# Zero rows for the last token block of attention, and a new order of work, in an attention and two-MLP kernel

## The chip, the cores and the metric

The kernel runs on one core of a Trainium2 chip. The metric is the time of one execution on the device, in microseconds (us), the median of several runs.

## What is computed

Forgetting attention on 4 batches, 8 heads, 576 tokens and 64 dimensions a head, then two MLPs on the 2304 tokens:

```python
scores = scale * np.matmul(q, k.transpose(0, 1, 3, 2))
cum = np.cumsum(np.log(np.clip(f, 0.0001, 1.0)), axis=-1)
scores = np.where(causal, -1000000000.0, scores + cum[:, :, :, None] - cum[:, :, None, :])
attn = np.exp(scores - np.max(scores, axis=-1, keepdims=True))
attn = attn / (np.sum(attn, axis=-1, keepdims=True) + 1e-09)
x = np.matmul(attn, v)                                    # to 2304 tokens x 512
h = x @ w_in;   x = (np.maximum(h, 0) + alpha * np.minimum(h, 0)) @ w_out
h = x @ w_in2;  x = (np.maximum(h, 0) + np.log1p(np.exp(-np.abs(h)))) @ w_out2
```

The MLPs are 512 to 2048 to 512. All is float32; the kernel splits operands into a high and a low float32r part and adds three products.

## The kernel before

576 tokens are four blocks of 128 and one of 64. Heads are taken two at a time, so a pair (`pairs`, 16 of them) fills 128 partitions. For each pair SP loads q, k and v by token blocks (`load_tok`, L468 and L472, where L472 brings the last block, into rows 0 to 63). `transposed` (L497) turns q and k, in two halves (`prep_q`, `prep_k`): blocks 0 and 1, then blocks 2, 3 and the short one, whose transpose reads 64 rows. GpSimd makes the high and low parts of v (`prep_v`, L558 and L562). `query_tile` takes 64 queries of both heads: the decay on GpSimd (L578), scores on TensorE (L592; for the first eight pairs in float32, with a mask product L595), row maximum on VectorE (L601), exponential on ScalarE (L614), the transposes of the probabilities (L625) and their high (ScalarE, L641) and low parts (VectorE, L645), which lie in blocks of the tiles `PT` (p00, p01, p10, p11, with h or l). `values` multiplies them by v (L680), for queries 0 to 255 and 256 to 575 and for each head: token block by token block, the high part and then the low one. In the second of these the last two of ten products read the short block, again 64 rows. `finish` divides by the sums and hands the result on, through DRAM for batches 2 and 3 (L744).

The MLPs work on six chunks of 384 tokens. `hidden` (L816) makes 128 rows of h with 12 products, `product` (L873) multiplies by w_out, `weights` loads (L382, L387, or a saved copy, L368) and splits the weights on ScalarE and VectorE (L390 to L416). Chunks 0 to 2 (batches 0 and 1) are worked on with the first MLP beside the last eight pairs; at the end of attention (`switch2`) its memory becomes that of chunks 3 to 5, which `fetch` brings from DRAM (L776: x3h, x4h, x5h and x3l, x4l, x5l).

The order of all work comes from a planner, `Plan`: each step is added with its engine, an assumed length, what it reads and writes, and a rank; `emit` plays the steps through and gives each engine, of those that are ready, the one of least rank. The ranks come from the numbers in `TUNE`: a unit per query tile (`TILE1`, `TILE2`), per MLP slot (`SLOT2`, `SLOT3`), and offsets for each kind of step, one for the first eight pairs and one for the last eight. The program then holds a fixed order on each engine; waits between engines are by semaphores.

## Time and profile before

| | us |
|---|---|
| median of 3 runs (lowest, highest) | 1051.91 (1050.93, 1052.27) |
| the profiled execution | 1050.04 |
| its span in the profile | 1048.1 |
| TensorE (PE) busy | 1036.1 (99%) |
| VectorE (DVE) busy | 731.8 (70%) |
| ScalarE (ACT) busy | 539.0 (51%) |
| GpSimd (POOL) busy | 220.8 (21%) |

Busy times are unions over the whole span; what they mean is seen only by stages, as the shares differ between attention alone, attention beside the first MLP, and the MLPs alone. In a timeline the start of a TensorE instruction is recorded, its end is modelled, and neighbours overlap: what an instruction costs is read from the distance between its start and the next one.

### The profile page before, as it was taken

How to read it: one execution, taken by the hardware profiler on the slowest of the kernel's cores; microseconds unless marked ns; L12 is line 12 of the kernel's file. 1: busy time of each engine (PE TensorE's matmuls, PEld its weight loads, DVE VectorE, ACT ScalarE, POOL GpSimd, SP SyncE). 2: the span in 40 equal slices, each digit the busy share in tenths (PEclk: the TensorE clock that was granted, in tenths of full speed). 3: DMA queues.
4: the chain of work that ended last, by engine and by line, in shares of the span. 5: the costliest groups of instructions: out<-in, count | busy, mean ns of one | idle time of the engine just before them, and what ended most of it. 6: DMA issues, size and time to landing. Idle time of an engine off the chain costs nothing.

```text
span 1048.1 us, 16749 instructions
## 1 busy us (share of the span) xinstructions
PE 1036.1 (99%) x5852; PEld 955.9 (91%) x5852; DVE 731.8 (70%) x1664; ACT 539.0 (51%) x1312; POOL 220.8 (21%) x399
## 2 busy tenths in 40 slices
PE   8999999999999999999999999999999999999998
PEld 6777779999999999999999999999999999999997
DVE  6899888897999887532334669736954895495453
ACT  6899887777777654443333356334522442242221
POOL 6787755564345410000000000000000000000000
PEclk8999999999999999999999999999999999999999
DMA  6656345554564359003131203101300130010111
GB/s 147 145 143 182 92 138 161 173 171 139 171 194 144 103 155 300 2 11 111 61 121 61 81 1 101 61 1 33 114 16 1 42 105 15 1 41 3 58 52 69
DMA packets 125923, 97.49 MB, mean 93 GB/s; under 512 B 82496, under 2 KB 103120, under 8 KB 125840
## 3 DMA queue, kind: packets, MB, share of 16 engines
q1 hardware_dynamic: 125840, 96.43, 31.2%
q8 instruction: 46, 0.75, 0.3%
q14 instruction: 37, 0.30, 0.1%
HBM read 74.24 MB, written 22.17 MB: 92 GB/s over the span
## 4 chain that ended last, share of the span: by engine, by line
PE 92%; DVE 4%; ACT 2%; issue 1%; DMA 1%; POOL 0%; SPq 0%; DVEq 0%; ACTq 0%
PE h L816 37%; PE o L873 37%; PE pt L592 6%; PE pt L680 5%; PE pt L625 4%; PE pt L497 1%; DVE d L601 0%; DMA raw<-in_moe_w_in_dram 0%; ACT p L614 0%; DVE p01l L645 0%; DVE ca L405 0%; ACT qw L538 0%; DVE ca L401 0%; DMA kr<-in_k_dram 0%; DVE acc L894 0%
## 5 line engine op out<-in xcount | busy, mean ns | idle before, releaser
L873 PE MATMUL o<-g,wout 128*128 128x384 f32 x1152 | 214.9, 336 | 0.2 <-DVE x4l L905 0.2
L873 PE MATMUL o<-wout,g 128*128 128x512 f32 x864 | 214.5, 393 | 0.0
L873 PEld LDWEIGHTS o<-g,wout 128*128 128x128 f32 x1152 | 199.9, 188 | 1.0 <-DVE x4l L905 0.5
L873 PEld LDWEIGHTS o<-wout,g 128*128 128x128 f32 x864 | 160.8, 188 | 29.4
L855 DVE TENSOR_TENSOR g<-h,g 128x384 fp32r<-128x384 f32 x192 | 106.5, 555 | 56.0 <-ACT g L852 55.5
L842 ACT ACTIVATE ta<-ta 128x384 f32<-128x384 f32 x96 | 50.4, 525 | 175.2 <-DVE ta L838 175.1
L852 ACT CAST g<-h 128x384 fp32r<-128x384 f32 x192 | 92.0, 480 | 91.0 <-DVE h L845 52.4
L829 DVE SCALAR_TENSOR_TENSOR h<-ta,slope,h 128x384 f32<-128x384 f32 x96 | 59.4, 618 | 77.2 <-ACT h L826 77.0
L578 POOL TENSOR_SCALAR d<-cumb,cumc 128x64 f32<-128x64 f32 (+2 forms) x144 | 91.5, 640 | 101.6 <-ACT p L614 88.2
L838 DVE TENSOR_SCALAR ta<-h 128x384 uint32<-128x384 uint32 x96 | 53.3, 555 | 69.7 <-PE h L816 69.6
L823 ACT ACTIVATE ta<-h 128x384 f32<-128x384 f32 x96 | 47.1, 491 | 105.0 <-PE h L816 104.2
L614 ACT ACTIVATE p<-d,mx 128x64 f32<-128x64 f32 (+2 forms) x144 | 80.9, 562 | 13.2 <-DVE mx L601 12.2
L894 DVE TENSOR_TENSOR acc<-o,acc 128x512 f32<-128x512 f32 (+1 forms) x102 | 62.7, 622 | 20.3 <-PE o L873 18.3
L845 DVE SCALAR_TENSOR_TENSOR h<-h,ta 128x384 f32<-128x384 f32 x96 | 54.0, 563 | 31.6 <-ACT ta L842 31.6
L601 DVE CUSTOM_DVE_ANT_0 d<-pt,d 128x64 f32<-128x64 f32 (+2 forms) x144 | 63.3, 450 | 7.9 <-PE pt L592 2.2
L625 PE MATMUL pt<-ident,p 128*128 128x128 f32 (+1 forms) x400 | 64.3, 281 | 2.3 <-DVE p01l L645 0.8
L625 PEld LDWEIGHTS pt<-ident,p 128*128 128x128 f32 (+1 forms) x400 | 45.1, 140 | 12.7 <-ACT p L614 4.1
L816 PE MATMUL h<-x0h,win 128*128 128x384 f32 x256 | 55.5, 339 | 0.0
L816 PE MATMUL h<-x1h,win 128*128 128x384 f32 x256 | 55.4, 339 | 0.0
L816 PE MATMUL h<-x2h,win 128*128 128x384 f32 x256 | 55.2, 338 | 0.0
L816 PE MATMUL h<-x5h,win 128*128 128x384 f32 x256 | 54.9, 335 | 0.0
L816 PE MATMUL h<-x4h,win 128*128 128x384 f32 x256 | 54.9, 335 | 0.0
(138 smaller groups left out, 1966.8 us busy)
## 6 DMA issues: line engine op xcount, KB each, us to landing
raw<-in_moe_w_in_dram SPq DMA_DIRECT2D x32, 512.0 KB, 4.6
raw<-in_moe_w_out_dram SPq DMA_DIRECT2D x32, 512.0 KB, 3.5
rb<-rd SPq DMA_DIRECT2D x32, 144.0 KB, 3.7
out_dram<-acc SPq DMA_DIRECT2D x18, 256.0 KB, 2.0
cumb<-cum_d SPq DMA_DIRECT2D x30, 144.0 KB, 3.3
qr<-in_q_dram SPq DMA_DIRECT2D x32, 128.0 KB, 2.5
kr<-in_k_dram SPq DMA_DIRECT2D x32, 128.0 KB, 2.5
vr<-in_v_dram SPq DMA_DIRECT2D x32, 128.0 KB, 3.6
```

What stands on the lines that cost most here:

```text
L578: nc.gpsimd.tensor_scalar(out=buf(dk)[:, 0:w], in0=buf(cb)[:, 0:w], scalar1=-1.0, scalar2=cumc[:, t, i:i + 1], op0=ALU.mult, op1=ALU.add,)
L592: nc.tensor.matmul(out=buf(key)[:, 0:c1 - c0], lhsT=a[:, t, :], rhs=b_[:, c0:c1], start=(s == 0), stop=(s == len(products) - 1 and not mas ...
L601: nc.vector.tensor_tensor_reduce(out=d[:, c0:c1], in0=buf(key)[:, 0:c1 - c0], in1=d[:, c0:c1], scale=-1.0, scalar=least, op0=ALU.add, op1= ...
L614: nc.scalar.activation(out=buf(pk)[:, 0:w], in_=buf(dk)[:, 0:w], func=AF.Exp, bias=buf(mk)[:, x:x + 1], scale=-1.0, accum_out=buf(sm)[:, t ...
L625: nc.tensor.transpose(out=buf(tk[x])[0:rows, (j - j0) * 128:(j - j0) * 128 + 128], in_=buf(pk)[:, j * 128:j * 128 + rows], identity=ident,)
L816: nc.tensor.matmul(out=hb(), lhsT=w_[:, kk * 128:kk * 128 + 128], rhs=x_[:, kk, :], start=(s == 0), stop=(s == len(ops) - 1))
L829: nc.vector.scalar_tensor_tensor(out=hb(), in0=buf(ka), scalar=slope[:, ff:ff + 1], in1=hb(), op0=ALU.mult, op1=ALU.add)
L845: nc.vector.scalar_tensor_tensor(out=hb(), in0=hb(), scalar=0.0, in1=buf(ka), op0=ALU.max, op1=ALU.add)
L852: nc.scalar.copy(out=buf(kg)[0], in_=hb())
L855: nc.vector.tensor_sub(buf(kg)[1], hb(), buf(kg)[0].bitcast(F32))
L873: nc.tensor.matmul(out=buf(ok)[:, 0:width], lhsT=a, rhs=b_, start=(j == 0 and s == 0), stop=(j == G - 1 and s == 2))
L894: nc.vector.tensor_add(buf(ok)[:, 0:width] if inner else ac(), buf(ok)[:, 0:width], ac())
```

## The change

The short block is filled up: rows 64 to 127 of the last block of the loaded q and k, as before of v, and of the block of `PT` that holds the short block's probabilities are set to zero once, at the start; loads and evictions only ever write rows 0 to 63 there. The transposes of q and k and the value products then read 128 rows for every block. The transpose of the short block writes 128 columns, of which 64 are read on. The planner's assumed lengths of transposes, scores and value products are altered, and all numbers of `TUNE` are new, so most steps stand elsewhere in each engine's order.

```diff
-    "TILE1": 0.34, "TILE2": 2.84, "SLOT2": 14.32, "SLOT3": 1.72, "qr": (-39.24, -10.94), "kr": (-19.35, 4.31),
...
+    "TILE1": 2.64, "TILE2": 2.56, "SLOT2": 25.17, "SLOT3": 1.95, "qr": (-2.51, -15.17), "kr": (3.69, -1.2),
...
@@ transposed
         for c in range(c0, c1):
-            n = min(128, S - c * 128)
             nc.tensor.transpose(
-                out=p[:, c * 128 - t0:c * 128 - t0 + n],
-                in_=src[0:n, c].rearrange("p h d -> p (h d)"),
-                identity=ident[0:n, 0:n],
+                out=p[:, c * 128 - t0:c * 128 - t0 + 128],
+                in_=src[:, c].rearrange("p h d -> p (h d)"),
+                identity=ident,
             )
@@ prep_k, and the same in prep_q
-        plan.add("pe", (c1 - c0) * 0.1075, lambda: transposed(pk, buf(rk), hf), writes=[pk] + ([key] if hf == 0 else []),
-                 reads=[rk, ("ident",)] + ([key] if hf else []), rank=rank)
+        plan.add("pe", (c1 - c0) * 0.109 + 0.04, lambda: transposed(pk, buf(rk), hf), writes=[pk] + ([key] if hf == 0 else []),
+                 reads=[rk, ("ident",), ("vz",)] + ([key] if hf else []), rank=rank)
@@ query_tile
-        plan.add("pe", sum(t_f32(c1 - c0) if whole(i) else 3 * t_mm(c1 - c0) for c0, c1 in cuts) + 0.06 * whole(i), scores,
+        plan.add("pe", sum(t_f32(c1 - c0) if whole(i) else 3 * t_mm(c1 - c0) for c0, c1 in cuts) + 0.06 * whole(i) + 0.04, scores,
...
-            plan.add("pe", (j1 - j0) * 0.1075, lambda x=x: turn(x), reads=[pk], writes=[tk[x], region], rank=R(n + due("turn", i)))
+            plan.add("pe", (j1 - j0) * 0.109 + 0.04, lambda x=x: turn(x), reads=[pk], writes=[tk[x], region], rank=R(n + due("turn", i)))
@@ values
                 for s, (j, x, c0) in enumerate(mm):
-                    rows = min(128, S - j * 128)
                     b0, nt = block((i0 + c0) // 64, j), (w - c0) // 64
                     nc.tensor.matmul(
                         out=buf(pk)[:, c0:w],
-                        lhsT=buf(vk)[0:rows, j, h].rearrange("p a d -> p (a d)"),
-                        rhs=PT[home(i)][g][x][0:rows, b0:b0 + nt, h, :],
+                        lhsT=buf(vk)[:, j, h].rearrange("p a d -> p (a d)"),
+                        rhs=PT[home(i)][g][x][:, b0:b0 + nt, h, :],
...
-            plan.add("pe", sum(t_mm(w - c0) for _, _, c0 in mm), pe, rank=R(n0 + h),
-                     reads=[vk] + regions + ([] if g == h == 0 else [yk]),
+            plan.add("pe", sum(t_mm(w - c0) for _, _, c0 in mm) + 0.04, pe, rank=R(n0 + h),
+                     reads=[vk, ("pz",)] + regions + ([] if g == h == 0 else [yk]),
@@ setup
-        plan.add("pool", 0.15, lambda: zero(tiles["vr", 0][64:128, NJ - 1]), writes=[("vz",)], rank=R(-8))
+        for x in ("qr", "kr", "vr"):
+            plan.add("pool", 0.15, lambda x=x: zero(tiles[x, 0][64:128, NJ - 1]), writes=[("vz",)], rank=R(-8))
+        for n in range(2):
+            for x in range(2):
+                plan.add("pool", 0.15, lambda n=n, x=x: zero(PT[n][1][x][64:128, 15].bitcast(F32)), writes=[("pz",)], rank=R(-6))
```

Three places show what moved.

TensorE, late in the first pair and early in the second (L497 becomes L496: transposes of q and k; L625 becomes L624: of probabilities; L592 becomes L591: scores). Before:

```order
L625 MATMUL pt5_0_156<-ident_60,p3_0_150 128x128 x4
L592 MATMUL pt7_0_158<-kw0_0_161,qw0_0_159 128x384
L595 LDWEIGHTS identb_61
L595 MATMUL pt7_0_158<-maskb_63,identb_61 128x64
L497 MATMUL pt0_0_116<-ident_60,qr0_0_124 128x128 x2
L625 MATMUL pt1_0_117<-ident_60,p0_0_110 128x128 x2
L497 MATMUL pt2_0_118<-ident_60,kr0_0_125 128x128 x2
L497 MATMUL pt4_0_155<-ident_60,qr0_0_124 128x128 x2
L497 MATMUL pt4_0_155<-ident_60,qr0_0_124 128x64
L497 MATMUL pt3_0_119<-ident_60,kr0_0_125 128x128 x2
L497 MATMUL pt3_0_119<-ident_60,kr0_0_125 128x64
```

and now, a little earlier in the first pair:

```order
L624 MATMUL pt5_0_156<-ident_60,p3_0_150 128x128
L591 MATMUL pt6_0_157<-kw0_0_161,qw0_0_159 128x512
L594 LDWEIGHTS identb_61
L594 MATMUL pt6_0_157<-maskb_63,identb_61 128x64
L496 MATMUL pt7_0_158<-ident_60,qr0_0_124 128x128 x2
L624 MATMUL pt0_0_116<-ident_60,p0_0_110 128x128
L591 MATMUL pt1_0_117<-kw0_0_161,qw0_0_159 128x256
L594 LDWEIGHTS identb_61
L594 MATMUL pt1_0_117<-maskb_63,identb_61 128x64
L496 MATMUL pt2_0_118<-ident_60,qr0_0_124 128x128 x3
L624 MATMUL pt4_0_155<-ident_60,p1_0_111 128x128 x4
```

The transposes of the second pair's q stand between the first pair's scores instead of behind them, and the second half is three full transposes instead of two and one of 64 columns.

SP, at the end of attention: the last two stores to DRAM (L744, now L742), the fetch of chunks 3 to 5 (L776, now L774) and weight loads. Before, and then now:

```order
L744 DMA xb_dh_67<-rb0_0_134 128x576
L744 DMA xb_dl_68<-x320_0_107 128x576
L368 DMA win5_0_4721<-w_dh_69 128x512
L368 DMA win5_1_4722<-w_dl_70 128x512
L776 DMA x3h_4711<-xb_dh_67 128x4x384
L776 DMA x4h_4713<-xb_dh_67 128x4x192 x2
L776 DMA x5h_4715<-xb_dh_67 128x4x384
L382 DMA raw1_0_84<-in_moe2_w_in_dram 128x4x128
L368 DMA wout0_0_1863<-w_dh_69 128x512
L368 DMA wout0_1_1864<-w_dl_70 128x512
L776 DMA x3l_4712<-xb_dl_68 128x4x384
L368 DMA wout1_0_1865<-w_dh_69 128x512
```

```order
L742 DMA xb_dh_67<-rb0_0_134 128x576
L742 DMA xb_dl_68<-x320_0_107 128x576
L382 DMA raw1_0_84<-in_moe2_w_in_dram 128x4x128
L368 DMA win5_0_4889<-w_dh_69 128x512
L368 DMA win5_1_4890<-w_dl_70 128x512
L774 DMA x3h_4879<-xb_dh_67 128x4x384
L774 DMA x4h_4881<-xb_dh_67 128x4x192 x2
L774 DMA x5h_4883<-xb_dh_67 128x4x384
L368 DMA wout5_0_4891<-w_dh_69 128x512
L368 DMA wout5_1_4892<-w_dl_70 128x512
L774 DMA x3l_4880<-xb_dl_68 128x4x384
L774 DMA x4l_4882<-xb_dl_68 128x4x192 x2
```

A load of w_in2 (L382) now stands between the stores and the first fetch, and one pair of w_out loads instead of a w_in2 load and a pair between x5h and x3l. That load needs its buffer raw1 free of an earlier read, which is the last of these rows of VectorE (the L689 are the sums of the last value products, L405 the read of raw1; the L892 add results of TensorE):

```order
L689 TENSOR_TENSOR x320_0_107<-pt2_0_118,xt_133 64x320
...
L689 TENSOR_TENSOR x320_0_107<-pt0_0_116,xt_133 64x320
L853 TENSOR_TENSOR g4_1_1893<-h0_0_1898,g4_0_1892 128x384
L827 SCALAR_TENSOR_TENSOR h1_0_1899<-ta1_0_1897,slope_64,h1_0_1899 128x384
L393 TENSOR_SCALAR cu0_0_87<-ca0_0_85 128x512
L892 TENSOR_TENSOR o0_0_1900<-o0_0_1900,acc0_1881 128x384
L397 SCALAR_TENSOR_TENSOR cu0_0_87<-raw1_0_84,cu0_0_87 128x512
L853 TENSOR_TENSOR g5_1_1895<-h1_0_1899,g5_0_1894 128x384
L892 TENSOR_TENSOR o1_0_1901<-o1_0_1901,acc0_1881 128x384
L401 TENSOR_SCALAR ca0_0_85<-raw1_0_84 128x512
L405 SCALAR_TENSOR_TENSOR ca0_0_85<-ca0_0_85,raw1_0_84 128x512
```

GpSimd, at the start, behind the mask (the first decays are L578, now L577; L558 and L562 become L557 and L561). Before, and then now, with some rows of the zeroing left out of the second:

```order
L976 MEMSET vr0_0_126 64x128
L976 MEMSET qw0_0_159 128x1152
L976 MEMSET qw1_0_160 128x1152
L976 MEMSET q0_0_120 128x1152
L976 MEMSET q0_1_121 128x1152
L610 MEMSET p3_0_150 128x64
L558 TENSOR_SCALAR v0_0_106<-vr0_0_126 128x5x64
L578 TENSOR_SCALAR d3_0_148<-cumb0_0_105,cumc_65 128x64
L578 TENSOR_SCALAR d0_0_108<-cumb0_0_105,cumc_65 128x128
L578 TENSOR_SCALAR d1_0_109<-cumb0_0_105,cumc_65 128x576
```

```order
L974 MEMSET qr0_0_124 64x128
L974 MEMSET qw0_0_159 128x1152
L974 MEMSET kr0_0_125 64x128
L974 MEMSET p01h_114 64x128
...
L974 MEMSET q0_1_121 128x1152
L557 TENSOR_SCALAR v0_0_106<-vr0_0_126 128x5x64
L609 MEMSET p3_0_150 128x64
L561 TENSOR_TENSOR v0_0_106<-vr0_0_126,v0_0_106 128x5x64
L557 TENSOR_SCALAR v0_0_106<-vr0_0_126 128x5x64
L561 TENSOR_TENSOR v0_0_106<-vr0_0_126,v0_0_106 128x5x64
L577 TENSOR_SCALAR d3_0_148<-cumb0_0_105,cumc_65 128x64
```

Six memsets are added, and all of the first pair's v work stands ahead of the first decays. In SP's queue the first pair's v is now loaded before its k.

## Rows read from the trace of the kernel before

**Rows 1.** The page, busy time of the engines and share of the span.

```profile
PE 1036.1 (99%) x5852; PEld 955.9 (91%) x5852; DVE 731.8 (70%) x1664; ACT 539.0 (51%) x1312; POOL 220.8 (21%) x399
```

**Rows 2.** Busy times by stretch; the second number of an engine counts its instructions.

```profile
core 0: us, PE busy (x) PEld busy (x) DVE busy (x) ACT busy (x) POOL busy (x), PEclk, DMA share, GB/s
0.00:26.00 26.00, 23.35 (x129) 17.62 (x130) 16.98 (x52) 16.20 (x45) 16.02 (x38) 0.87 0.63 147
26.00:131.00 105.00, 102.63 (x654) 79.39 (x652) 94.36 (x295) 93.88 (x284) 83.08 (x144) 1.00 0.56 141
76.80:92.40 15.60, 14.77 (x95) 11.33 (x96) 14.88 (x47) 14.59 (x44) 13.09 (x23) 1.00 0.67 182
131.00:145.00 14.00, 11.60 (x71) 9.02 (x69) 12.17 (x38) 10.80 (x33) 9.70 (x20) 1.00 0.51 141
145.00:384.00 239.00, 238.44 (x1500) 228.01 (x1499) 214.36 (x537) 176.01 (x457) 108.68 (x196) 1.00 0.53 155
```

**Rows 3.** Order of time on PE, end of a group of value products: start, length, instruction.

```profile
62.89 0.27 PE L680 MATMUL pt<-p01l,v 128*128 128x192 f32 x1
63.09 0.29 PE L680 MATMUL pt<-p01h,v 64*128 64x64 f32 x1
...
63.43 0.41 PE L680 MATMUL pt<-p01h,v 128*128 128x320 f32 x1
63.68 0.30 PE L680 MATMUL pt<-p01l,v 128*128 128x320 f32 x1
```

**Rows 4.** Order of time on PE, three 64-column products with 128 rows.

```profile
183.30 0.50 PE L592 MATMUL pt<-k,q 128*128 128x64 f32 x3
183.64 0.60 PE L816 MATMUL h<-x1h,win 128*128 128x384 f32 x2
```

**Rows 5.** Order of time on PE, transposes of q and k, then value products.

```profile
67.22 0.38 PE L497 MATMUL pt<-ident,qr 128*128 128x128 f32 x2
67.44 0.38 PE L497 MATMUL pt<-ident,kr 128*128 128x128 f32 x2
67.66 0.58 PE L497 MATMUL pt<-ident,qr 128*128 128x128 f32 x3
68.17 0.64 PE L497 MATMUL pt<-ident,kr 128*128 128x128 f32 x3
68.75 0.39 PE L680 MATMUL pt<-p10h,v 128*128 128x256 f32 x1
68.97 0.28 PE L680 MATMUL pt<-p10l,v 128*128 128x256 f32 x1
...
69.26 0.33 PE L680 MATMUL pt<-p10h,v 128*128 128x256 f32 x1
69.43 0.28 PE L680 MATMUL pt<-p10l,v 128*128 128x256 f32 x1
```

**Rows 6.** Groups by line and shape, the 64-row forms on PE.

```profile
L680 PE MATMUL pt<-p01h,v 64*128 64x64 f32 x24 | 7.1, 294 | 0.0
...
L497 PE MATMUL pt<-ident,kr 64*128 64x64 f32 x16 | 4.4, 273 | 0.0
...
L680 PE MATMUL pt<-p11h,v 64*128 64x64 f32 x8 | 2.4, 294 | 0.0
```

**Rows 7.** Order of time on POOL, the first work on v.

```profile
8.61 0.46 POOL L558 TENSOR_SCALAR v<-vr 128x320 fp32r<-128x320 f32 x1 [1.69 <-DMA vr<-in_v_dram]
```

**Rows 8.** Order of time on PE: first k transposes, last value product, first on x3.

```profile
9.00 0.86 PE L497 MATMUL pt<-ident,kr 128*128 128x128 f32 x5
...
383.76 0.27 PE L680 MATMUL pt<-p01l,v 64*128 64x64 f32 x1
...
434.01 0.85 PE L816 MATMUL h<-x3h,win 128*128 128x384 f32 x4
```

**Rows 9.** SP's queue in order of time, and DMA issues with us to landing.

```profile
402.18 0.54 SPq L776 DMA_DIRECT2D x3l<-xb_dl  x1
...
x3l<-xb_dl SPq DMA_DIRECT2D x1, 768.0 KB, 10.0
```

## What the change should do to the time

> **What bounds the kernel now.** I read the busy line of the page first: TensorE is busy 1036.1 of 1048.1 us [rows 1]. Then the busy times by stretch, which show three regimes [rows 2]. From 26 to 131 us attention runs alone: PE 102.63 of 105 us, but DVE 94.36 and ACT 93.88 stand close behind. From 131 to 145 us, between the last attention-only pair and the first MLP products, PE is busy 11.60 of 14 us. From 145 to 384 us attention and the first MLP run side by side and PE has 238.44 of 239 us; DVE has 214.36 there. A busy PE is not a PE at its peak, so the third view is the order of time, read by the distances between starts.
>
> In the value products the last 192-column product starts at 62.89, the first product with 64 rows at 63.09, the first with 128 rows after the two at 63.43, its successor at 63.68 [rows 3]. So the product ahead of the change of rows holds PE for 0.20 us, the two 64-row products for 0.34, and the one after the change for 0.25. With 128 rows throughout, three 64-column products take 0.34 us together (183.30 to 183.64), that is 0.11 each [rows 4]. In the transposes two full ones take 0.22 us (67.22 to 67.44), 0.11 each; a group of three whose last has 64 rows takes 0.51 (67.66 to 68.17) and, behind another such group, 0.58; the value product after it has 0.22 to its successor where the same product elsewhere has 0.17 [rows 5]. So what costs time is the entering and leaving of the 64-row form, about 0.1 us each way, plus a few hundredths in the instruction behind it.
>
> **The change, part by part.**
>
> *Value products.* Each group of ten ends with two 64-row products; the counts of the high parts are 24 and 8, so 32 groups [rows 6]. From 62.89 to 63.68 a group now takes 0.79 us. Changed: three at 0.11, and the first of the next group at 0.17 to 0.25 [rows 5, 3]; I take 0.19, nearer to the 0.17 of a first product that has no change of rows ahead of it, and a little more because 320 columns are not 256. That is 0.52, a gain of 0.27 (0.21 to 0.29), and 32 times that is 8.6 us (6.7 to 9.3).
>
> *Transposes of q and k.* For each of 16 pairs the second half of q and of k ends with a 64-row transpose; k's row says 16 and q has as many, so 32 groups [rows 6]. With 128 rows and 128 columns a group costs 3 x 0.11 = 0.33 instead of 0.51 or 0.58, and the instruction behind it gets up to 0.05 back. I take 0.24, as most groups stand behind another or before a value product: 7.7 us (0.18 to 0.25: 5.8 to 8.0). The doubled columns of the last transpose cost nothing beyond this, since 0.11 is the price of a 128-column one.
>
> *Untouched.* The 64-column transposes of the probabilities and the MLP products keep their forms. From the first use of token chunk 3 on, PE's rows stand as before, so the last 610 us keep their length.
>
> Both gains are 16.3 us (12.5 to 17.3) of TensorE time. Some 30 of the 64 groups lie in 145 to 384 us, 28 in 26 to 131 us.
>
> *What DVE and ACT give back.* In 145 to 384 us some 7.7 us go and DVE would have 214.36 of 231.3, 93%, below the 95% (14.88 of 15.6 us) that it reached between 76.8 and 92.4 us [rows 2]; I count that gain whole. In 26 to 131 us 28 groups at 0.255 are 7.1 us, which leaves 97.9 us for DVE's 94.36: 96%, above anything seen. At 95% the stretch is 98.9 us long (1.0 given back), at today's 90% it stays 105 (7.1 given back). I take 94%, 100.4 us, so 2.5 us given back: nearest to the 95% stretch, since there too DVE was what PE stood behind. The late one is then the row maximum and the low parts of the probabilities on DVE.
>
> *Start.* The zeroing of q's, k's and four probability tiles comes before POOL's first v work, where POOL idles 1.69 us until v has landed at 8.61 us [rows 7]; six short memsets fit there, and without this cover they would move the first decays by about their own length. The load of k now stands behind that of v, so it lands when v did, at about 8.6; its transposes started at 9.00 [rows 8]. Neither should be late; I set 0.5 us for both (0 to 1.5, the second if the memsets and the earlier v work hold up the first decays after all).
>
> *The new order.* More than the padding moves: almost all of PE's rows up to 384 us stand elsewhere. PE's visible idle time up to 145 us is 2.65 + 2.37 + 2.40 = 7.4 us [rows 2]; a better order can take some of it, a worse one add to it. I set 0, with 2.6 us either way.
>
> *A rule weighed.* In the first 26 us the granted clock averaged 0.87, that is 3.4 us lost at the 1.2 GHz level; from 26 to 131 us it is 1.00 although transposes of q, k and the probabilities run throughout [rows 2]. The Trainium skill (TensorE: Matmul & The Clock Gate, Part 4: PE-mode transpose) says that transposes do not count as PE being busy for the clock. By that rule longer transposes, and the two groups of them that the order now puts between the first scores, would prolong the low level, at up to another 3.4 us. The trace speaks against it, with 1.00 beside hundreds of transposes, so the sum has nothing for it.
>
> *Sum.* 16.3 - 2.5 - 0.5 = 13.3 us. The profiled execution took 1050.0 us, so 1036.7 on its own scale; the median of the runs is 1.9 us higher, at 1051.9, which gives **1038.6 us**. A measurement of this kernel can tell about 0.2%, 2.1 us, from no change.
>
> **Rivals.**
>
> *DVE and ACT keep the attention-only part at its length.* For it: both are at 90% there and idle mostly on each other. Against it: the 95% stretch. Then 7.1 us are given back instead of 2.5: gain 8.7, 1043 us. Chance 0.18.
>
> *Nothing is given back and the order removes waits.* For it: 7.4 us of visible idle time up to 145 us. Against it: DVE would need 96% for 100 us. Gain 16.3 to 19.9, about 1034 us. Chance 0.13.
>
> *Low clock prolonged at the start*, by the rule above: 3.4 us less, 1042 us. Chance 0.03.
>
> *The price belongs to short products, not to the change of rows.* Then 64-column products with 128 rows cost the same and only a microsecond or two moves: about 1051 us, the same. Against it stand the 0.11 us of full-row 64-column products [rows 4]. Chance 0.04, with other ways to end within 0.2%.
>
> *Slower: the fetch of chunk 3 comes late.* Now the last value product starts at 383.76 and the first product on x3 at 434.01 [rows 8], with 288 MLP products between, 0.174 us each. The low part x3l is issued at 402.18 and takes 10.0 us [rows 9], so it is there 28.4 us after the last value product, 21.8 us before PE wants it. In the changed order 192 MLP products stand between: 33.5 us, which leaves 5.1. And in SP's queue a weight load that waits for DVE now stands ahead of these fetches; DVE's step that frees its buffer stands behind two additions that wait for 48 of those MLP products, 8.4 us. If x3l lands over 5 us later than now, PE stops for the excess; it takes 5.1 + 13.3 + 2.1 = 20.5 us of lateness to end slower than before by 0.2%, say 1055 us. Against it: one weight load that stood between x5h and x3l has gone ahead of x3h, so that x3l follows x5h sooner. Chance 0.04; a stop of a few microseconds lies inside the range.
>
> **How the numbers follow.** The forecast's own case, a gain between 10 and 16 us, gets 0.58. With the DVE rival, the full gain and the clock rule, faster is 0.92; same 0.04; slower 0.04. The range ends at the full 17.3 with 2.6 us from the order (1032.0), and at 12.5 with 6 us given back (1045.4).
>
> **What would show it.** The 64-row forms are gone from PE's groups; between the last 192-column value product and the second product after the group lie about 0.52 us, and a group of three transposes takes 0.33 us. Attention alone ends some 4 to 6 us earlier, with DVE near 94% in it; the last value product starts about 3 us later, since 96 more MLP products (16.7 us) stand ahead of it. No wait stands before the first product on x3. The forecast is wrong if PE's idle time up to 145 us grows by more than 7 us, if the groups keep more than 0.65 us, or if PE waits for x3.

## The result and the profile after

| | before | changed |
|---|---|---|
| median of 4 runs (lowest, highest), us | 1052.09 (1050.93, 1052.29) | 1042.03 (1040.70, 1043.41) |
| profiled execution, us | 1050.04 | 1040.70 |
| its span, us | 1048.1 | 1039.0 |

The ratio is 0.9911, 95% interval 0.9899 to 0.9924: 10.1 us faster by the medians, 9.1 us by the spans. The forecast of 1038.6 us is 3.4 us below the measured median.

The page's busy line of the changed kernel, beside [rows 1]:

```profile
PE 1020.6 (98%) x5852; PEld 948.8 (91%) x5852; DVE 732.5 (71%) x1664; ACT 536.5 (52%) x1312; POOL 225.2 (22%) x405
```

PE lost 15.5 us of busy time (1036.1 to 1020.6) with the same number of instructions, while the span lost 9.1. The difference, 6.4 us, is new idle time of PE. So the first question is where the idle time is. The busy times by stretch, in the stretches and columns of [rows 2]:

```profile
0.00:26.00 26.00, 22.55 (x133) 16.83 (x134) 18.53 (x57) 17.10 (x48) 20.39 (x48) 0.93 0.79 172
26.00:131.00 105.00, 98.83 (x687) 80.60 (x685) 97.52 (x309) 97.17 (x296) 81.00 (x148) 1.00 0.61 149
131.00:145.00 14.00, 12.00 (x77) 10.64 (x77) 11.45 (x32) 12.61 (x35) 8.27 (x18) 1.00 0.35 107
145.00:384.00 239.00, 236.14 (x1502) 227.50 (x1501) 215.71 (x532) 170.29 (x447) 112.28 (x191) 1.00 0.50 150
```

PE's idle time up to 145 us is 26.00 - 22.55, 105.00 - 98.83 and 14.00 - 12.00, together 11.6 us where it was 7.4. From 145 to 384 us it is 2.9 where it was 0.6. In the same 105 us from 26 on, 687 PE instructions run instead of 654.

Fixed stretches mix what moved. From here on I cut each trace at two points of the program: the first product of the first MLP, and the first product on x3. The stages are attention alone, attention beside the first MLP with its rest, and the MLPs alone. The busy times by stretch of the kernel before, cut so, and then of the changed one, the first two stages (columns as in [rows 2]):

```profile
0.00:144.90 144.90, 137.47 (x850) 105.97 (x850) 123.41 (x383) 120.78 (x359) 108.80 (x201) 0.98 0.57 142
144.90:434.00 289.10, 288.54 (x1787) 278.08 (x1787) 249.30 (x602) 198.91 (x506) 112.03 (x198) 1.00 0.53 161
```

```profile
0.00:138.30 138.30, 126.69 (x849) 101.41 (x849) 120.88 (x380) 120.23 (x359) 107.53 (x207) 0.99 0.62 149
138.30:425.30 287.00, 284.14 (x1790) 275.46 (x1789) 251.86 (x604) 196.80 (x506) 117.70 (x199) 1.00 0.53 162
```

The first stage lost 6.6 us, the second 2.1, and the third, from 614.1 to 613.7 us, 0.4. PE's busy time fell by 10.8 us in the first stage and by 4.4 in the second.

Two views show the mechanism itself. First the order of time on PE at the end of a group of value products, beside [rows 3] (L680 is L678 now):

```profile
74.20 0.27 PE L678 MATMUL pt<-p11l,v 128*128 128x192 f32 x1
74.31 0.22 PE L678 MATMUL pt<-p11h,v 128*128 128x64 f32 x1
74.36 0.28 PE L678 MATMUL pt<-p11l,v 128*128 128x64 f32 x1
74.47 0.36 PE L678 MATMUL pt<-p10h,v 128*128 128x256 f32 x1
74.67 0.28 PE L678 MATMUL pt<-p10l,v 128*128 128x256 f32 x1
```

From the last 192-column product to the second instruction behind the group lie 0.47 us (74.20 to 74.67), where it was 0.79. The three instructions ahead of the change of group take 0.27 (74.20 to 74.47), where it was 0.54 (62.89 to 63.43). Then the groups by line and shape, beside [rows 6]; no form with 64 rows is left at these two lines:

```profile
L496 PE MATMUL pt<-ident,kr 128*128 128x128 f32 x80 | 13.7, 284 | 0.0
...
L678 PE MATMUL pt<-p01h,v 128*128 128x64 f32 x24 | 5.2, 215 | 0.0
```

### The profile page after: what moved, and what is told of

It reads as the page before. It is cut to its first block, busy times and chain, and to the rows that moved or that the text cites. A ratio compares the mean times of both kernels' runs of the same rounds, so it can differ in the third digit from the quotient of the medians.

```text
span 1039.0 us, 16738 instructions
## 1 busy us (share of the span) xinstructions
PE 1020.6 (98%) x5852; PEld 948.8 (91%) x5852; DVE 732.5 (71%) x1664; ACT 536.5 (52%) x1312; POOL 225.2 (22%) x405
## 4 chain that ended last, share of the span: by engine, by line
PE 83%; DVE 7%; ACT 6%; issue 2%; DMA 1%; POOL 1%; SPq 0%; ACTq 0%; DVEq 0%; POOLq 0%
PE h L814 36%; PE o L871 36%; PE pt L591 4%; PE pt L678 3%; PE pt L624 2%; ACT p L613 2%; DVE d L600 1%; PE pt L496 1%; DVE p01l L644 1%; DVE cu L397 1%; ACT p01h L640 1%; ACT xt L686 0%; DVE x L689 0%; ACT qw L537 0%; DMA cumb<-cum_d 0%
## 5 line engine op out<-in xcount | busy, mean ns | idle before, releaser
L577 POOL TENSOR_SCALAR d<-cumb,cumc 128x64 f32<-128x64 f32 (+2 forms) x144 | 93.9, 658 | 89.4 <-ACT p L613 77.5
L892 DVE TENSOR_TENSOR acc<-o,acc 128x512 f32<-128x512 f32 (+1 forms) x102 | 62.5, 620 | 18.5 <-PE o L871 16.3
L624 PE MATMUL pt<-ident,p 128*128 128x128 f32 (+1 forms) x400 | 68.3, 280 | 5.0 <-ACT qw L537 1.1
L624 PEld LDWEIGHTS pt<-ident,p 128*128 128x128 f32 (+1 forms) x400 | 45.3, 139 | 17.5 <-ACT p L613 3.9
```

Of the source, the lines that this page charges most:

```text
L577: nc.gpsimd.tensor_scalar(out=buf(dk)[:, 0:w], in0=buf(cb)[:, 0:w], scalar1=-1.0, scalar2=cumc[:, t, i:i + 1], op0=ALU.mult, op1=ALU.add,)
L624: nc.tensor.transpose(out=buf(tk[x])[0:rows, (j - j0) * 128:(j - j0) * 128 + 128], in_=buf(pk)[:, j * 128:j * 128 + rows], identity=ident,)
L892: nc.vector.tensor_add(buf(ok)[:, 0:width] if inner else ac(), buf(ok)[:, 0:width], ac())
```

## The experiments

The first question was what the padding and the new order are worth apart. Later runs ask why they don't add up. Medians are in us; the kernel before ran beside each batch, with a median of 1051.05 beside the first four, 1051.09 beside the next four (half orders, less ACT, less DVE) and 1050.68 beside the last four. Stage lengths are from the one profiled execution of each kernel, which can differ from its median by up to some 2 us, and in three of them by 2.4, 2.5 and 4.1 (the new first half; padding in the old order, less ACT; the corrected lengths).

| kernel | median (lowest, highest) | ratio to before, 95% | stages 1, 2, 3 |
|---|---|---|---|
| before | 1052.09 (1050.93, 1052.29) | | 144.9, 289.1, 614.1 |
| changed | 1042.03 (1040.70, 1043.41) | 0.9911 (0.9899, 0.9924) | 138.3, 287.0, 613.7 |
| padding, old order | 1039.43 (1038.40, 1040.71) | 0.9890 (0.9876, 0.9903) | 140.0, 282.7, 614.2 |
| new order, no padding | 1045.07 (1045.01, 1046.34) | 0.9945 (0.9933, 0.9958) | 140.2, 289.5, 613.7 |
| transposes padded, old order | 1047.35 (1046.94, 1048.06) | 0.9967 (0.9955, 0.9979) | 143.3, 287.7, 614.1 |
| values padded, old order | 1042.97 (1042.68, 1044.69) | 0.9926 (0.9914, 0.9939) | 141.2, 285.8, 614.1 |
| new first half, old second | 1050.59 (1049.03, 1053.21) | 0.9997 (0.9988, 1.0006) | 134.7, 302.4, 614.1 |
| old first half, new second | 1055.73 (1054.34, 1056.44) | 1.0042 (1.0029, 1.0056) | 139.0, 299.5, 613.9 |
| changed, less ACT | 1036.48 (1036.32, 1036.75) | 0.9861 (0.9848, 0.9874) | 135.9, 285.5, 613.6 |
| changed, less DVE | 1038.49 (1037.81, 1039.71) | 0.9881 (0.9868, 0.9895) | 138.1, 286.2, 613.7 |
| changed, less ACT and DVE | 1033.42 (1032.87, 1033.78) | 0.9835 (0.9819, 0.9851) | 134.0, 283.5, 613.7 |
| padding, old order, less ACT | 1040.80 (1038.27, 1041.93) | 0.9901 (0.9886, 0.9916) | 137.9, 284.6, 614.1 |
| padding, old numbers, corrected lengths | 1057.86 (1057.58, 1061.96) | 1.0075 (1.0056, 1.0095) | 146.3, 299.9, 614.0 |
| padding, new numbers, old lengths | 1057.66 (1057.02, 1060.21) | 1.0069 (1.0054, 1.0084) | 138.6, 304.3, 613.6 |

### The padding alone

The changed kernel with the numbers and the assumed lengths of before, so that each engine's order is that of before plus six memsets:

```diff
-    "TILE1": 2.64, "TILE2": 2.56, "SLOT2": 25.17, "SLOT3": 1.95, "qr": (-2.51, -15.17), "kr": (3.69, -1.2),
+    "TILE1": 0.34, "TILE2": 2.84, "SLOT2": 14.32, "SLOT3": 1.72, "qr": (-39.24, -10.94), "kr": (-19.35, 4.31),
...
-        plan.add("pe", (c1 - c0) * 0.109 + 0.04, lambda: transposed(pk, buf(rk), hf), writes=[pk] + ([key] if hf == 0 else []),
+        plan.add("pe", (c1 - c0) * 0.1075, lambda: transposed(pk, buf(rk), hf), writes=[pk] + ([key] if hf == 0 else []),
...
-            plan.add("pe", sum(t_mm(w - c0) for _, _, c0 in mm) + 0.04, pe, rank=R(n0 + h),
+            plan.add("pe", sum(t_mm(w - c0) for _, _, c0 in mm), pe, rank=R(n0 + h),
```

> Padding alone: the transposes and value products read 128 rows, and every engine keeps the order of the kernel before (six memsets are added at the start). PE's own work should fall as in the changed kernel, by 15 to 17 us, if the price sits in the 64-row form. Theory A (DVE and ACT give the saving back, whatever the order): PE's waits grow by some 6 us here too, and the time is 1041 to 1044 us. Theory B (the new order makes waits of its own from 145 to 384 us): waits grow by under 4 us here, and the time is 1036 to 1040 us. Theory C (the padding needs the new order to pay): 1045 us or more.

Measured: 1039.43 us, 11.6 below before. Its busy times by stretch, the first two stages:

```profile
0.00:140.00 140.00, 130.01 (x849) 103.60 (x850) 123.39 (x381) 120.03 (x359) 109.97 (x207) 0.98 0.59 146
140.00:422.70 282.70, 281.55 (x1789) 275.34 (x1788) 249.02 (x604) 198.45 (x506) 113.20 (x198) 1.00 0.53 165
```

Here the second stage gives 6.4 us, where the changed kernel has 2.1, and the first gives 4.9. The order of time on PE, two groups of three transposes and the value products behind them, beside [rows 5]:

```profile
50.10 0.49 PE L496 MATMUL pt<-ident,qr 128*128 128x128 f32 x3
50.43 0.49 PE L496 MATMUL pt<-ident,kr 128*128 128x128 f32 x3
50.67 0.36 PE L678 MATMUL pt<-p00h,v 128*128 128x256 f32 x1
```

A group in front of another takes 0.33 (50.10 to 50.43), where it took 0.51, and one in front of a value product 0.24, where it took 0.58. So the padding alone explains the whole sign and more than the whole size of the result. It is also the fastest kernel here that leaves nothing out; its lead over the changed kernel (1.5 us by the gains, 2.6 by the medians) isn't settled, since the two intervals overlap between 0.9899 and 0.9903.

### The new order alone

The changed kernel with 64-row reads of the short block; the order is that of the changed kernel:

```diff
+            n = min(128, S - c * 128)
...
-                in_=src[:, c].rearrange("p h d -> p (h d)"),
-                identity=ident,
+                in_=src[0:n, c].rearrange("p h d -> p (h d)"),
+                identity=ident[0:n, 0:n],
...
-                        lhsT=buf(vk)[:, j, h].rearrange("p a d -> p (a d)"),
-                        rhs=PT[home(i)][g][x][:, b0:b0 + nt, h, :],
+                        lhsT=buf(vk)[0:min(128, S - j * 128), j, h].rearrange("p a d -> p (a d)"),
+                        rhs=PT[home(i)][g][x][0:min(128, S - j * 128), b0:b0 + nt, h, :],
```

> The new order alone: every engine's order as in the changed kernel, but the last block's transposes and value products read 64 rows. Theory A: the order is worth nothing by itself, 1050 to 1054 us. Theory B: the order costs by itself, 1054 to 1058 us. Theory C: the order gains by itself, 1045 to 1049 us.

Measured: 1045.07 us, 6.0 below before. Its busy times by stretch, the first two stages:

```profile
0.00:140.20 140.20, 134.61 (x849) 104.64 (x849) 120.53 (x380) 120.43 (x359) 106.12 (x207) 0.98 0.61 147
140.20:429.70 289.50, 288.85 (x1790) 278.28 (x1790) 252.24 (x604) 196.79 (x506) 116.85 (x199) 1.00 0.53 161
```

By itself the order takes 4.7 us off the first stage and nothing off the second. The four kernels stand crosswise: without padding the new order gains 6.0 us, with it it seems to lose about 2, which isn't settled; in the old order padding gains 11.6, in the new one 10.1 - 6.0 = 4.1. Yet PE has 12.7 us less to do in the changed kernel than in this one (1020.6 against 1033.3 busy). Two thirds of what the padding freed came back as PE waiting for others: its idle time is 18.4 us in the changed kernel and 10.1 in this one.

### The two kinds of products apart

Both in the old order. Transposes at 128 rows and values at 64:

```diff
-                        lhsT=buf(vk)[:, j, h].rearrange("p a d -> p (a d)"),
-                        rhs=PT[home(i)][g][x][:, b0:b0 + nt, h, :],
+                        lhsT=buf(vk)[0:min(128, S - j * 128), j, h].rearrange("p a d -> p (a d)"),
+                        rhs=PT[home(i)][g][x][0:min(128, S - j * 128), b0:b0 + nt, h, :],
```

> Old order, and only the transposes of q and k filled up; value products still read 64 rows. By the sum of the prediction PE's work falls by 7.7 us (5.8 to 8.0). All theories: the time falls by somewhat less, 4 to 7.5 us, 1044.5 to 1048 us; under theory B nearer to 7.

And the other way round:

```diff
+            n = min(128, S - c * 128)
...
-                in_=src[:, c].rearrange("p h d -> p (h d)"),
-                identity=ident,
+                in_=src[0:n, c].rearrange("p h d -> p (h d)"),
+                identity=ident[0:n, 0:n],
```

> Old order, and only the value products filled up; transposes still read 64 rows. By the sum of the prediction PE's work falls by 8.6 us (6.7 to 9.3). The time falls by 5 to 8.5 us, 1043.5 to 1047 us; under theory B nearer to 8, and with the transposes' gain it adds up to that of both.

Measured: 3.7 us off for the transposes, a little less than was expected, and 8.1 for the values, 11.8 together, as much as both at once (11.6). The values give their whole price: PE's busy time falls by 8.1 (1036.1 to 1028.0) and the time by 8.1. The transposes don't: busy time falls by 5.7 (to 1030.4), and the time by two thirds of that. PE's idle time grows by 2.7 us there, to 8.8 and 1.9 in the first two stages where it was 7.4 and 0.6.

### Less work on ACT and on DVE

If the changed kernel's PE waits for ACT and DVE, then taking work off them must shorten it although PE keeps all of its own. Less ACT: the row sums of the exponential are left out (their read-out goes too; ones stand in their place, written once at the start):

```diff
-                                 scale=-1.0, accum_out=buf(sm)[:, t:t + 1])
+                                 scale=-1.0)
...
```

> The changed kernel without the row sums of the exponential (the sums are left out and set to one, so the result is not divided by them): 144 reads of an accumulator, 0.19 us each, are gone from ScalarE, 1.7 us for each pair of 13, and every order stays. If PE stands behind ScalarE's load, PE's waits up to chunk 3 (28.5 us) fall by 5 us or more and the time is 1036 us or less. If it stands behind VectorE, or each step is late by its place in the order and not by an engine's load, the time falls by under 2 us.

Less DVE: two steps of the splitting of the weights work on half of their columns:

```diff
-            nc.vector.tensor_scalar(out=buf(ua).bitcast(U32), in0=parts()[1].bitcast(U32), scalar1=511, scalar2=None,
+            nc.vector.tensor_scalar(out=buf(ua)[:, 0:256].bitcast(U32), in0=parts()[1][:, 0:256].bitcast(U32), scalar1=511, scalar2=None,
...
-            nc.vector.scalar_tensor_tensor(out=buf(ua), in0=buf(ua).bitcast(U32), scalar=2.0 ** 32, in1=parts()[0],
+            nc.vector.scalar_tensor_tensor(out=buf(ua)[:, 0:256], in0=buf(ua)[:, 0:256].bitcast(U32), scalar=2.0 ** 32, in1=parts()[0][:, 0:256],
```

> The changed kernel with two of VectorE's steps on weights (the fraction and the low word) on half of their columns (the low parts of the weights are left unfinished in the other half): about 0.55 us less VectorE work for each of 64 weights, 2.7 us up to 131 us and some 15 us from there to 384 us, and every order stays. If PE stands behind VectorE's load, the stage beside the first MLP shortens by 2 to 4 us and the time is 1037 to 1040 us. If not, under 1 us.

And both edits in one kernel:

```diff
-                                 scale=-1.0, accum_out=buf(sm)[:, t:t + 1])
+                                 scale=-1.0)
...
-            nc.vector.tensor_scalar(out=buf(ua).bitcast(U32), in0=parts()[1].bitcast(U32), scalar1=511, scalar2=None,
+            nc.vector.tensor_scalar(out=buf(ua)[:, 0:256].bitcast(U32), in0=parts()[1][:, 0:256].bitcast(U32), scalar1=511, scalar2=None,
...
```

> The changed kernel with both reliefs, ScalarE without the row sums and VectorE with half of two weight steps. If the new order's waits beside the first MLP (9.4 us, against 5.6 in the old order) come from the two engines' load, they fall to 6 us or less and the span to 1032 us. If they come from where its steps stand, they stay at 7 us or more and the span is 1033 to 1035 us.

Each is set against the kernel before of its own batch, where the changed kernel's gain is 10.1 us. Less ACT (536.5 to 525.0 us busy) gains 14.6, less DVE (732.5 to 713.1) gains 12.6, both gain 17.3. So 4.5, 2.5 and 7.2 us come free with PE's work and its order unchanged. In the profile of less DVE, the slowest of its four executions, the second stage is only 0.8 us shorter than in the changed kernel, where 2 to 4 were expected; there the clock fell to 0.50 from 138.3 to 141.7 us, which can hide up to 1.7 us. The busy times by stretch of the kernel with both edits, the first two stages:

```profile
0.00:134.00 134.00, 127.22 (x848) 102.66 (x849) 118.00 (x380) 113.48 (x280) 106.89 (x209) 1.00 0.64 153
134.00:417.50 283.50, 282.07 (x1791) 275.83 (x1790) 243.25 (x604) 192.01 (x441) 113.78 (x199) 1.00 0.53 164
```

The second stage is 3.5 us shorter than in the changed kernel, near the 282.7 of padding in the old order, and PE's idle time in it halves, 2.9 to 1.4. In the first stage, 4.3 us shorter, it falls from 11.6 to 6.8. The clock at the start can't explain that: counted as in the last section, its low level lasted 14.4 us here and 9.3 there. That PE in the changed kernel waits for DVE and ACT together, in both stages, is shown by this. How it comes about is seen in the trace of the changed kernel. First PE's waits from 140 to 330 us there (line, what it waited for, us in total, times, longest):

```profile
PE pt L591 <- DVE x L689: 0.5, 1, 0.5
PE pt L496 <- DVE p01l L644: 0.4, 1, 0.4
PE pt L624 <- DVE p01l L644: 0.4, 1, 0.4
PE pt L624 <- DVE k L514: 0.2, 1, 0.2
PE pt L591 <- DVE k L514: 0.2, 1, 0.2
PE pt L591 <- DVE mx L600: 0.2, 1, 0.2
PE h L814 <- DVE g L853: 0.2, 1, 0.2
PE pt L624 <- ACT p L613: 0.2, 1, 0.2
```

The same view of padding in the old order has two rows:

```profile
PE h L814 <- DVE g L853: 0.6, 2, 0.4
PE pt L624 <- ACT p L613: 0.2, 1, 0.2
```

No single wait does it. Eight places each wait a few tenths, seven of them for DVE: 2.3 us in these rows against 0.8. The two second stages differ by 4.3 us, 1.7 of it in PE's idle time (2.9 against 1.1) and 2.6 in its busy time (284.14 against 281.55 with the same products). Most of that busy time was waiting as well, in pieces that the modelled ends cover: with less ACT and DVE, in the same order on PE, it is 282.07. The longest wait in the order of time, PE first:

```profile
185.44 1.07 PE L624 MATMUL pt<-ident,p 128*128 128x128 f32 x7
187.05 0.73 PE L591 MATMUL pt<-k,q 128*128 128x512 f32 x2 [0.53 <-DVE x L689]
```

then DVE,

```profile
186.50 0.49 DVE L689 TENSOR_TENSOR x<-pt,xt 64x320 f32<-64x320 f32 x1 [0.34 <-ACT xt L686]
```

and ACT:

```profile
185.48 0.46 ACT L613 ACTIVATE p<-d,mx 128x192 f32<-128x192 f32 x1
185.84 0.19 ACT L613 ACTIVATION_READ_ACCUMULATOR p<-d,mx 128x1 f32 x1
186.05 0.42 ACT L686 COPY xt<-pt 64x320 f32<-64x320 f32 x1
```

The scores wait for a PSUM buffer that DVE's sum of the value products (L689) frees. DVE waited 0.34 us for the copy on ACT (L686), which stands behind an exponential and its read-out of the row sum, the very read-out that the kernel with less ACT leaves out. The groups of DVE from 138 to 425 us show where it is late (busy and mean ns, then idle time before them and who ended it), in the changed kernel

```profile
L600 DVE CUSTOM_DVE_ANT_0 d<-pt,d 128x384 f32<-128x384 f32 (+8 forms) x64 | 28.2, 450 | 4.1 <-POOL d L583 2.4 <-PE pt L591 1.2 <-issue 0.3
...
L412 DVE TENSOR_SCALAR cu<-cu 128x512 uint32<-128x512 uint32 x28 | 13.2, 473 | 4.6 <-ACT win L409 3.0 <-ACT wout L409 1.5
```

and with padding in the old order:

```profile
L600 DVE CUSTOM_DVE_ANT_0 d<-pt,d 128x320 f32<-128x320 f32 (+8 forms) x65 | 28.8, 451 | 1.1 <-PE pt L591 0.7 <-issue 0.2
...
L412 DVE TENSOR_SCALAR cu<-cu 128x512 uint32<-128x512 uint32 x28 | 11.8, 425 | 0.8 <-ACT win L409 0.8
```

DVE is 88% busy in the second stage of both kernels (251.86 of 287.0, 249.02 of 282.7). But in the new order the row maximum stands where the decay from POOL isn't ready (2.4 us), and a weight step where ACT isn't (4.5 us). In sum DVE's idle time is nearly the same in both, 35.1 and 33.7 us: the rows show the places, not the cost.

Would the same relief shorten the old order too? The padding alone, with the row sums left out:

```diff
-                                 scale=-1.0, accum_out=buf(sm)[:, t:t + 1])
+                                 scale=-1.0)
...
```

> Padding with the old order, without the row sums of the exponential (left out and set to one): the same relief of ScalarE as in the changed kernel, where it gave 4 us. If both orders stand equally behind ScalarE, the span falls by 3 to 5 us here too, to 1032 to 1034 us, and the two orders stay 2 us apart. If the new order's second stage alone stands behind ScalarE, under 2.5 us come here.

Measured: 1040.80 us, a gain of 9.9 where the padding alone gained 11.6, with runs 3.7 us apart: no shorter. In its profile, the fastest of the four executions and 2.5 us below their median, the first stage is 2.1 us shorter, although the low clock at the start lasted 2 us longer (13.2 against 11.2), and the second 1.9 longer. So by the medians the relief of ACT is worth something in the new order only. Why the second stage of the old order lengthens with less work isn't settled, and DVE's relief was not tried there.

### The order in halves, and its numbers without its lengths

If stages were independent, the new numbers for the first eight pairs and the old ones for the rest would join the shorter first stage with the shorter second:

```diff
-    "TILE1": 2.64, "TILE2": 2.56, "SLOT2": 25.17, "SLOT3": 1.95, "qr": (-2.51, -15.17), "kr": (3.69, -1.2),
...
+TUNE = {'TILE1': 2.64, 'TILE2': 2.84, 'SLOT2': 14.32, 'SLOT3': 1.72, 'qr': (-2.51, -10.94), 'kr': (3.69, 4.31), ...
...
-        plan.add("pe", (c1 - c0) * 0.109 + 0.04, lambda: transposed(pk, buf(rk), hf), writes=[pk] + ([key] if hf == 0 else []),
+        plan.add("pe", (c1 - c0) * (0.109 if whole(i) else 0.1075) + 0.04 * (whole(i)), lambda: transposed(pk, buf(rk), hf), writes=[pk] + ([key] if hf == 0 else []),
...
```

> Both paddings; the numbers and assumed lengths of the new order for the first eight pairs, those of the order before for the last eight and the MLPs. If the stages add (new order up to the first MLP product 136.8 us, old order from there to the first use of chunk 3 282.7 us, the rest 609.9 us), the span is 1035 us and the time 1036 to 1038 us, below padding alone. If the second stage's waits depend on how the first one ends, or belong to the padding whatever the order, it is 1039 to 1043 us.

The reverse takes the numbers and lengths of the first half from before and those of the second from the change:

```diff
-    "TILE1": 2.64, "TILE2": 2.56, "SLOT2": 25.17, "SLOT3": 1.95, "qr": (-2.51, -15.17), "kr": (3.69, -1.2),
...
+TUNE = {'TILE1': 0.34, 'TILE2': 2.56, 'SLOT2': 25.17, 'SLOT3': 1.95, 'qr': (-39.24, -15.17), 'kr': (-19.35, -1.2), ...
...
```

> Both paddings; the old order's numbers for the first eight pairs, the new order's for the rest. If the stages add (138.6, 287.1 and 609.4 us), the span is 1041 us and the time 1042 to 1044 us, the slowest of the padded ones, and PE's waits from the first MLP product to chunk 3 are about 10 us as in the changed kernel. If the loss is not the new order's in that stage, 1037 to 1040 us.

Measured: 1050.59 and 1055.73 us, 11 and 16 above padding in the old order and well outside all that was expected of either. The first has the shortest first stage of all kernels whose work is whole (134.7 us), and then a second stage of 302.4 us, 15 longer than the changed kernel's and 20 longer than that of padding in the old order. A half of either order couldn't be taken over. Two more kernels keep one of the two parts of the change whole. The changed kernel with the old numbers, and so with corrected lengths alone:

```diff
-    "TILE1": 2.64, "TILE2": 2.56, "SLOT2": 25.17, "SLOT3": 1.95, "qr": (-2.51, -15.17), "kr": (3.69, -1.2),
+    "TILE1": 0.34, "TILE2": 2.84, "SLOT2": 14.32, "SLOT3": 1.72, "qr": (-39.24, -10.94), "kr": (-19.35, 4.31),
...
```

> Both paddings and the corrected lengths, but the old numbers, so the planner lays out a third order. If corrected lengths by themselves let the planner fit the work to the engines, waits stay below padding alone and the time is 1035 to 1039 us. If numbers and lengths only belong together (as the mixed numbers suggest), waits up to chunk 3 rise to 30 us or more and the time is 1043 to 1056 us.

And the changed kernel with the old assumed lengths:

```diff
-        plan.add("pe", (c1 - c0) * 0.109 + 0.04, lambda: transposed(pk, buf(rk), hf), writes=[pk] + ([key] if hf == 0 else []),
+        plan.add("pe", (c1 - c0) * 0.1075, lambda: transposed(pk, buf(rk), hf), writes=[pk] + ([key] if hf == 0 else []),
...
-            plan.add("pe", sum(t_mm(w - c0) for _, _, c0 in mm) + 0.04, pe, rank=R(n0 + h),
+            plan.add("pe", sum(t_mm(w - c0) for _, _, c0 in mm), pe, rank=R(n0 + h),
```

> Both paddings and the new numbers, but the old lengths. If the numbers belong to the lengths, waits rise and the time is 1044 to 1056 us; if the lengths hardly matter to the order, the time is that of the changed kernel, 1040 to 1043 us.

Measured: 1057.86 and 1057.66 us, about 7 us slower than the kernel before, with all of the padding in, and 2 us beyond the slower of the two outcomes expected of each. Hundredths of a microsecond in assumed lengths give orders 17 to 19 us apart (7.0 lost against 10.1 gained, 7.2 against 11.6). So the numbers fit the lengths with which they were found, and neither is better by itself. What such an order costs shows in the last of these, its busy times by stretch around 130 us:

```profile
120.00:132.80 12.80, 10.91 (x76) 8.99 (x75) 12.26 (x34) 9.41 (x29) 11.25 (x20) 1.00 0.47 134
132.80:143.10 10.30, 7.89 (x25) 6.19 (x24) 6.92 (x17) 5.03 (x15) 5.24 (x8) 0.50 0.42 134
```

PE is idle for 1.9 of 12.8 us, in part here (order of time on PE):

```profile
132.02 0.30 PE L624 MATMUL pt<-ident,p 128*128 128x128 f32 x1 [1.24 <-DVE mx L600]
```

and then for 10.3 us its granted clock is 0.50, the 1.2 GHz level, in which only 25 of its instructions run. The lost clock follows the idle time and is the smaller part: 10.3 us at half speed cost 5.2 us at most, a second fall of 3.4 us at 252 us another 1.7, and the first two stages together are 20.2 us longer than with padding in the old order (442.9 against 422.7).

## Why the prediction was right, and which step failed

- **Value products, 8.6 us.** Right. Over all 32 groups, the time from the start of the last 192-column product to the start of the instruction behind the two 64-column ones is 17.3 us before (0.54 each), 8.8 in the changed kernel (0.27 each) and 9.0 with padding in the old order, where one group waits. Padded alone the values were worth 8.1 us of time.
- **Transposes, 7.7 us.** The price was a little high and the time it bought far too high. Over all 32 groups of three, from the first start to the start behind the group, it is 17.7 us before and 10.8 with padding in the old order: 6.8, or 0.21 a group where I had 0.24. Padded alone they brought only 3.7 us; much of the rest went into waits (2.7 us more idle time on PE). In the changed kernel the groups still take 13.9 us, since waits stand inside some of them (the longest group takes 1.40).
- **Attention alone gives back 2.5 us.** Right in size for the order that I had read: with padding in the old order PE's busy time falls by 7.5 us in the first stage and the time by 4.9, so 2.6 come back. I had 4 to 6 us off the end of attention alone; in the changed kernel the stage is 6.6 shorter, of which up to 1.9 is the clock at the start. What DVE and ACT hold back there is real: with their work reduced the stage is 4.3 us shorter still, although the low clock lasted 5.1 us longer. I placed DVE at 94% from 26 to 131 us; it is 93% (97.52 of 105).
- **"I count that gain whole", 145 to 384 us, 7.7 us.** This step failed. The second stage gave 2.1 us in the changed kernel. It gives 6.4 with the same padding in the old order, so the size was right for the order that I had read. I argued that DVE stayed below the 95% it had once reached. But DVE's share is 88% in both kernels. A share below a ceiling says that the work fits, not that each result is there when a fixed order wants it.
- **The new order, 0 with 2.6 us either way.** This step had the wrong form. The order is worth -6.0 us without the padding, beyond the bounds, and perhaps +2 with it, from shorter first stages and a second stage that can't use what the padding frees. No fixed number for the order, added to the gain of the padding, gives both.
- **Start, 0.5 us.** Within its bounds: PE's idle time up to 26 us grew by 0.8 us (23.35 to 22.55 busy), with four more instructions run. The zeroing alone can't be seen to cost PE anything: with the values padded in the old order, which has the same six memsets, PE is busy for 23.53 of the 26 us with 132 instructions.
- **Clock.** I read the 0.87 over the first 26 us as 3.4 us lost. That was a misreading, since the view counts the time before its first clock record as full speed, and PE ran at the low level there too (last section). By the distances between starts the low level lasted 13.1 us before and 9.3 in the changed kernel, which is at most 1.9 us of time in its favour. The Trainium skill (TensorE: Matmul & The Clock Gate, Part 4: PE-mode transpose) says that transposes don't count as PE being busy for the clock in the way other products do. By that rule the low level should have grown, and it did not; in the same order with 64-row reads it lasted 12.7 us. With padding in the old order the clock even rose at 4.4 us, behind the fourteenth of the 18 transposes with which PE starts and before it had done anything else. The rule's rival did not occur.
- **Short products instead of the change of rows.** Excluded: the same 64-column products with full rows cost half, 0.27 us for three where it was 0.54.
- **The late fetch.** The path was as I described it, and the slack was enough. The last value product starts 8.1 us later than before where I had 3; that is the 16.7 us of extra MLP products less the 8.7 us gained ahead of it. The rows of the changed kernel, beside [rows 8, 9]:

```profile
391.85 0.28 PE L678 MATMUL pt<-p01l,v 128*128 128x64 f32 x1
...
425.32 0.85 PE L814 MATMUL h<-x3h,win 128*128 128x384 f32 x4
426.02 0.68 PE L814 MATMUL h<-x3l,win 128*128 128x384 f32 x3
```

```profile
410.21 0.53 SPq L774 DMA_DIRECT2D x3l<-xb_dl  x1
```

x3l is issued 18.4 us after the last value product, as before (402.18 - 383.76), and the products on chunk 3 follow 33.5 us after it with no wait ahead of them. DVE's step on raw1 held nothing up.

The forecast's total of 13.3 us was thus nearer to the padding alone (11.6 us) than to the change (10.1). That the measured time lies inside the range is in part luck. The range reached down to a gain of 6.5 us because it allowed for 6 us given back, which I had looked for in attention alone. The first stage gave about a microsecond more than I had reckoned; the second gave 5.6 less, and for that stage I had allowed nothing.

## What to carry to other kernels

A short block that uses half of the rows can cost more than a full one: price a form by the distances between starts around it, its entry and its exit included, before taking fewer rows as less work. Where the order on each engine is fixed, a cheaper instruction pays only as far as its neighbours on other engines are early enough, and a busy share below its ceiling doesn't show that; try the cheaper instruction in the old order before looking for a new one. Numbers that rank the work belong to the lengths they were found with, and here halves of two good orders made a bad one.

## What was not expected of the hardware

The clock's record says too little of the start. Over the first 26 us the view gives 0.87 in eight profiles, 0.93 in the changed kernel and 1.00 in five: transposes padded in the old order, the new first half, the new numbers with old lengths, and the two kernels that pair less ACT with less DVE or with the old order. The 1.00 is not full speed. First the order of time on PE with the padding alone, and one of its stretches:

```profile
1.43 3.59 PE L981 MATMUL pt<-ident 128*128 128x128 f32 x18 [1.43 <-POOL ident L952]
6.38 0.77 PE L496 MATMUL pt<-ident,qr 128*128 128x128 f32 x5
8.97 1.33 PE L496 MATMUL pt<-ident,kr 128*128 128x128 f32 x5
7.80:14.50 6.70, 6.56 (x27) 4.88 (x26) 3.30 (x13) 3.32 (x11) 4.92 (x11) 0.50 0.89 212
```

Then the same with less ACT, where PE has the same order:

```profile
1.43 4.10 PE L981 MATMUL pt<-ident 128*128 128x128 f32 x18 [1.43 <-POOL ident L952]
6.59 1.33 PE L496 MATMUL pt<-ident,qr 128*128 128x128 f32 x5
9.21 1.33 PE L496 MATMUL pt<-ident,kr 128*128 128x128 f32 x5
0.00:13.20 13.20, 11.33 (x55) 9.51 (x56) 6.47 (x16) 5.48 (x11) 10.48 (x31) 1.00 0.62 157
```

With the padding alone five transposes take 0.77 us at full speed and 1.33 at 0.50. With less ACT both groups take 1.33 in a stretch that is given as 1.00. The first clock record stands at 13.2 us there, and the view counts what lies before it as full. In all fourteen profiles transposes that follow each other ahead of the first record start 0.21 us apart, and 0.11 apart in stretches whose record gives full speed. Counted so, the low level lasted 9.3 us at the start of the changed kernel, 13.1 before, 12.7 with the new order and no padding, 11.2 with the padding alone, 13.2 with less ACT in the old order and 14.4 with less ACT and DVE. It is 11.2 or 13.2 us for the same order on PE, so it differs between executions. From 9.3 to 14.4 is up to 2.6 us of time, and first stages of single profiles should not be compared more finely than that.

In all four badly ordered kernels, and in the changed kernel with less DVE, the granted clock fell to the 1.2 GHz level again in the middle of the work. In the one shown PE had been idle for some of the time before, and the low level lasted 10.3 us from 132.8 on.
